# Talking-heads attention and a two-layer feed-forward: VectorE's order in an attention step, block timing, and where 48 weight pieces are decoded

## The chip, the cores and the metric

The kernel runs on one core of one Trainium2 chip, in one launch. The metric is the device time of that launch in microseconds; the lower the better. Each run also leaves a profile of one execution, taken on the same core.

## What is computed

```python
# q, k, v: (4, 12, 448, 64); w_pre, w_post: (12, 12)
scores = np.matmul(q, k.transpose(0, 1, 3, 2)) / np.sqrt(64)
scores = np.einsum('bhij,hg->bgij', scores, w_pre)
scores = scores - np.max(scores, axis=-1, keepdims=True)
attn = np.exp(scores)
attn = attn / (np.sum(attn, axis=-1, keepdims=True) + 1e-09)
attn = np.einsum('bhij,hg->bgij', attn, w_post)
out = np.matmul(attn, v)
x = out.transpose(0, 2, 1, 3).reshape(1792, 768)
h = x @ w_in                                   # w_in: (768, 2048)
g = np.where(h > 0, h, np.exp(np.minimum(h, 0)) - 1)
y = g @ w_out                                  # w_out: (2048, 768)
```

The two feed-forward weights arrive as 64-bit floats, the rest as 32-bit floats.

## The kernel before

**Attention.** The 448 query rows of a batch are cut into four blocks of 9, 12, 12 and 12 groups of 10 rows. With 12 heads, one group fills 120 partitions, so that the mixing over heads (w_pre, w_post) is a 120 x 120 product. Steps `j` take two groups each: a block is 5 or 6 steps, and 92 steps make the four batches. In one pass of the loop over `j` these things are issued, in the order in which they stand in the code, and each engine works through its own share in that order (the attention is under `manual_schedule`):

- `norm` for the step that was scored one pass earlier: the reciprocal of the sums on VectorE (L210, L211, tile `rz`) and two scalings of w_post on GpSimd (L215, tile `wz`).
- `scores` for step `j + 2`: two products `s` (L198) from the block's `raw` tile, VectorE's maxima `nm` (L200), ScalarE's exponentials `p` with their sums (L202).
- on some passes a *unit*: the q x k products of two head pairs for a coming block (L179), copied by ScalarE and VectorE into `st` (L187) and sent by a DMA into that block's `raw` tile, which changes the layout (L189). A block needs three units. `AHEAD` says how many steps ahead of the block's first scores its last unit stands.
- on some passes `av`: the products with v of a block that is already normalised (L249), and VectorE's copy `x` of the result (L261); the third one's DMA writes the block to DRAM (`xd`, L265).
- `post` for step `j`: two products with `wz` (L224, tile `t`), copied by ScalarE into `at` (L235).
- `dec.step()`: one of four VectorE operations of the weight decoder (below).
- work that is planned for this pass: loads of q, k and v, and their split into a high and a low part (L148, L149, L160, L161).

**Decoder.** Class `Weights` turns a 64-bit float into a 32-bit one by integer operations, in pieces of 128 x 512 numbers; 24 pieces make w_in (`s1`) and 24 make w_out (`s2`). A piece takes a load (`w`, L54), four VectorE operations in four calls of `step` (L68, L71, L77, L80), one ScalarE square (L75), and a store into DRAM (L84). The first `EARLY` pieces are decoded in the attention, where GpSimd issues the DMAs, the others in the feed-forward, where SyncE does.

**Feed-forward.** Two halves of 896 tokens. In each half the first products run over 16 slices `f` of the 2048 hidden columns and two groups of 448 tokens `u`, which gives 32 *units* of 18 products of 128 x 128 by 448 (L397). VectorE, ScalarE and VectorE again make the activation (L401, L403, L404, L405, L406), and ScalarE and GpSimd split it into `gh` and `gl` (L407, L408). The second products `y` follow (L445): 12 groups of 48. For every `f` and every group the weights are loaded from DRAM (L382), split by ScalarE into `hi` (L384) and by GpSimd into `lo` (L385). Before the first unit the tokens are loaded (`xl`, L367) and split into `xh` and `xl` (L369, L370). The decoder's calls stand in the first half only. The feed-forward is not under `manual_schedule`: the compiler's scheduler orders its instructions on each engine, and the order in the code is only its input.

Of the kernel before, what the change touches and what calls it, by code (L numbers as in the profile page):

```python
# [27 lines left out]
NC = DM // 128  # L28
PW = 512
EPS = 1e-9  # L30
EARLY = 22
LATE = 2


def f32(ap):
# [58 lines left out]
def body(ctx, tc, qd, kd, vd, wpre, wpost, w1d, w2d, outT):  # L94
# [5 lines left out]
    with tc.manual_schedule():  # L100
        attention(tc, qd, kd, vd, wpre, wpost, xd, todo[:EARLY])
    moe(tc, xd, s1, s2, todo[EARLY:], outT)


@with_exitstack
def attention(ctx, tc, qd, kd, vd, wpre, wpost, xd, todo):
    nc = tc.nc
# [18 lines left out]
    dec = Weights(ctx, tc, todo, nc.gpsimd)  # L126

    blocks = [(b, i) for b in range(B) for i in range(NB)]
    NBL = len(blocks)
# [4 lines left out]
    first = [steps.index((n, [0, 1])) for n in range(NBL)]  # L134
    length = [(c + 1) // 2 for c in count]
# [16 lines left out]
    def load_q(n, eng):  # L152
        q2[n] = ld.tile([128, NP, 120], F32, tag="q2", name="q2")
        eng.dma_start(out=q2[n], in_=qd[blocks[n]])

    def split_q(n, high, low):
        src = q2.pop(n)
        qh = qp.tile([128, NP, 120], F32R, tag="qh", name="qh")
        ql = qp.tile([128, NP, 120], F32R, tag="ql", name="ql")
        high(qh, src)  # L160
        low.tensor_sub(ql, src, f32(qh))  # L161
        qs[n] = qh, ql

    def load_v(b, hp):
        vs[b, hp] = vp.tile([128, NJ, 128], F32, tag="v", name="v")[:CJ]
        nc.gpsimd.dma_start(out=vs[b, hp], in_=vd[b, hp])
# [16 lines left out]
    def keep_qk(n, hp, got):  # L183
        m = count[n] * R
        for hh, copy in enumerate((nc.scalar.copy, nc.vector.tensor_copy)):
            st = stp.tile([120, S], F32, tag="st", name="st")
            copy(st[:m], got[hh][:m, :S])  # L187
            eng = nc.gpsimd if n == 0 and hh else nc.sync
            eng.dma_start(out=raws[n][2 * hp + hh:RH:H, :count[n], :], in_=st[:m])  # L189
# [17 lines left out]
    def norm(got, z):  # L207
        k = len(got)
        rz = small.tile([RH, 2], F32, tag="rz", name="rz")
        nc.vector.tensor_scalar_add(rz[:, :k], z[:, :k], EPS)  # L210
        nc.vector.reciprocal(rz[:, :k], rz[:, :k])  # L211
        out = []
        for i, p in enumerate(got):
            wz = small.tile([RH, RH], F32, tag="wz", name="wz", bufs=5)
            nc.gpsimd.tensor_scalar_mul(wz, wb, rz[:, i:i + 1])  # L215
            out.append((p, wz))
        return out
# [59 lines left out]
    wb = cst.tile([RH, RH], F32, name="wb")  # L277
    nc.sync.dma_start(out=wa, in_=wpre)
    nc.sync.dma_start(out=wb, in_=wpost)
    load_q(1, nc.sync)  # L280
    split_q(0, nc.scalar.copy, nc.vector)
    for hp in range(NP + 1):
        if hp < NP:
            split_k(0, hp, nc.scalar.copy, nc.vector)
        if hp:
            keep_qk(0, hp - 1, qk(0, hp - 1))
    nc.vector.tensor_scalar_mul(wa, wa, 1.0 / float(np.sqrt(D)))
    split_q(1, nc.vector.tensor_copy, nc.gpsimd)

    LOOK = 2
    AHEAD = 2
    work, units, avs = {}, {}, {}

    def plan(j, f):
        work.setdefault(max(j, -LOOK), []).append(f)

    for n in range(1, NBL):
        b, i = blocks[n]  # L300
        at = [max(first[n] - LOOK - AHEAD - (2 - u) * length[n - 1] // 3, -LOOK) for u in range(3)]
        for u in range(3):
            units.setdefault(at[u], []).append((n, u))
        if n > 1:
            plan(at[0] - 6, lambda n=n: load_q(n, nc.gpsimd))
            plan(at[0] - 2, lambda n=n: split_q(n, nc.vector.tensor_copy, nc.gpsimd))
        if i == NB - 1 and b + 1 < B:
            for hp in range(NP):
                plan(at[hp // 2] - 3 + hp % 2, lambda b=b + 1, hp=hp: load_k(b, hp, nc.gpsimd))
                plan(at[hp // 2] + hp % 2, lambda b=b + 1, hp=hp: split_k(  # L310
                    b, hp, nc.vector.tensor_copy, nc.gpsimd))
    for n in range(NBL):
        b, i = blocks[n]
        for u in range(3):
            j = first[n] + length[n] + (u * length[n + 1] // 3 if n + 1 < NBL else u)
            avs.setdefault(j, []).append((n, u))
            if i == NB - 1 and b + 1 < B:
                for hp in (2 * u, 2 * u + 1):
                    plan(j + 1, lambda b=b + 1, hp=hp: load_v(b, hp))
    for hp in range(NP):  # L320
        plan(hp - 1, lambda hp=hp: load_v(0, hp))

    sc, nz = {}, {}
    for j in range(-LOOK, N + 3):
        if j + LOOK - 1 in sc:
            nz[j + LOOK - 1] = norm(*sc.pop(j + LOOK - 1))
        if 0 <= j + LOOK < N:
            sc[j + LOOK] = scores(*steps[j + LOOK])
        for n, u in units.get(j, ()):
            got = [qk(n, hp) for hp in (2 * u, 2 * u + 1)]  # L330
            for w in range(2):
                keep_qk(n, 2 * u + w, got[w])
        for n, u in avs.get(j, ()):
            for w in range(2):
                av(n, 2 * u + w)
            keep_av(n, u)
        if j in nz:
            keep_post(*steps[j], post(nz.pop(j)))
        if j >= LATE:
            dec.step()  # L340
        for f in work.get(j, ()):
            f()
    while dec.step():
# [4 lines left out]
def moe(ctx, tc, xd, s1, s2, todo, outT):  # L348
    nc = tc.nc
# [10 lines left out]
    dec = Weights(ctx, tc, todo, nc.sync)  # L360
# [59 lines left out]
    for half in range(2):  # L420
        if half == 0:
            ahead(0)
        xs = [load_x(2 * half + u) for u in range(2)]
        for f in range(NF):
            ahead(i + 1)
            wh, wl = ready.pop(i)
            i += 1
            for u in range(2):
                up(f, u, wh, wl, *xs[u])
            if half == 0:  # L430
                dec.step(5)
        for m in range(NC):
            y = [ps.tile([128, 512], F32, tag="ps", name="y")[:, :S] for u in range(2)]
            for e in range(2):
                if half == 0:
                    dec.step(5 if m < NC - 2 else 64)
                ahead(i + 1)
                wh, wl = ready.pop(i)
                i += 1
                for u in range(2):  # L440
                    for k in range(8):
                        f = e * 8 + k
                        ks = slice(k * 128, (k + 1) * 128)
                        for n, (w, g) in enumerate(((wh, gh), (wl, gh), (wh, gl))):
                            nc.tensor.matmul(  # L445
                                y[u], w[:, ks], g[f][:, u, :],
                                start=f == 0 and n == 0, stop=f == NF - 1 and n == 2)
            for u in range(2):
                o = op.tile([128, S], F32, tag="o", name="o")
                nc.scalar.copy(o, y[u])  # L450
                nc.sync.dma_start(
                    out=outT[m * 128:(m + 1) * 128, (2 * half + u) * S:(2 * half + u + 1) * S],
                    in_=o)
# [46 lines left out]
```

## Time and profile before

| | |
|---|---|
| device time, median of 3 runs | 1026.11 us (1019.07 to 1030.36) |
| profiled execution, its own time | 1019.95 us, span 1018.2 us |
| mean granted TensorE clock | 0.976 of full speed |
| busy: TensorE, VectorE, ScalarE, GpSimd | 940.9, 523.9, 475.5, 416.5 us |
| attention | about 0 to 505 us |
| first half: first products, second products | about 506 to 661, 661 to 781 us |
| second half: first products, second products | about 781 to 898, 898 to 1014 us |

A line of a group names the source line, engine and operation, then what is written from what is read with the shape, how often it stands there, the busy time, the mean of one, and the idle time of that engine just before it with what ended most of it. The products are pipelined and their ends are modelled, so a single product's duration is longer than its share of a train; the share is read from the length of the train.

### The profile page before, as it was taken

What the parts mean: (1) busy time and instruction counts of PE and PEld (TensorE: products, weight loads), DVE (VectorE), ACT (ScalarE), POOL (GpSimd) and SP (SyncE); (2) the same over time, 40 slices, a digit from 0 to 9 for tenths busy, and PEclk for the clock granted to TensorE, in tenths of its full rate; (3) what the DMA queues carried; (4) which work ended last, traced back from release to release, by engine and by line L of the source; (5) the groups of instructions that cost most, each with busy time, mean ns of one, the idle gap of its engine ahead of it and who ended that gap; (6) DMA issues with size and microseconds to landing.
All of it is one profiled execution on the core that took longest, in us unless ns stands there. A gap on an engine that the chain in (4) does not pass through costs nothing.

```text
span 1018.2 us, 17108 instructions
## 1 busy us (share of the span) xinstructions
PE 940.9 (92%) x6216; PEld 775.3 (76%) x6216; DVE 523.9 (51%) x957; ACT 475.5 (47%) x988; POOL 416.5 (41%) x443
## 2 busy tenths in 40 slices
PE   4899999999999998999889888899999999999998
PEld 1576776677766666667778777789999999999997
DVE  3465665665556665555489999981001555530000
ACT  3465565565656565565545444552111555531110
POOL 2445434463445533333225444453222565641220
PEclk8899999999999999999989889999999999999999
DMA  5655436653565434642555455572221212122120
GB/s 178 193 170 163 140 127 191 188 181 119 174 215 173 145 126 159 201 140 83 151 191 182 156 171 170 178 210 94 80 81 62 62 47 63 52 71 89 62 87 28
DMA packets 78361, 136.30 MB, mean 134 GB/s; under 512 B 22894, under 2 KB 51890, under 8 KB 78278
## 3 DMA queue, kind: packets, MB, share of 16 engines
q1 hardware_dynamic: 68230, 101.23, 31.4%
q0 software_dynamic: 9504, 33.07, 10.6%
q8 instruction: 50, 0.82, 0.3%
q10 hardware_dynamic: 544, 0.92, 0.2%
q14 instruction: 33, 0.27, 0.1%
HBM read 72.86 MB, written 23.62 MB: 95 GB/s over the span
## 4 chain that ended last, share of the span: by engine, by line
PE 73%; DVE 14%; DMA 5%; issue 4%; ACT 3%; POOL 1%; SPq 0%; DVEq 0%; ACTq 0%; POOLq 0%
PE y L445 22%; PE s L198 13%; PE t L224 12%; PE h L397 12%; PE t L249 7%; PE qk L179 7%; DMA raw<-st 4%; DVE c L71 2%; DVE g L405 2%; DVE c L68 2%; DVE c L77 2%; DVE g L406 1%; DVE c L80 1%; DVE g L401 1%; ACT at L235 1%
## 5 line engine op out<-in xcount | busy, mean ns | idle before, releaser
L385 POOL TENSOR_TENSOR lo<-lo,hi 128x768 fp32r<-128x768 f32 (+1 forms) x56 | 119.4, 2134 | 205.3 <-ACT hi L384 205.1
L224 PEld LDWEIGHTS t<-wz,p 120*112 120x112 f32 x1440 | 158.4, 177 | 39.7 <-issue 35.0
L215 POOL TENSOR_SCALAR wz<-wb,rz 120x120 f32<-120x120 f32 x180 | 108.1, 609 | 182.7 <-DVE rz L211 174.9
L224 PE MATMUL t<-wz,p 120*112 120x120 f32 x1440 | 170.8, 270 | 12.6 <-ACT at L235 12.6
L198 PE MATMUL s<-raw,wa 120*120 120x448 f32 x360 | 156.1, 556 | 25.8 <-DMA raw<-st 11.2
L200 DVE TENSOR_REDUCE nm<-s 120x1 f32<-120x448 f32 x180 | 112.0, 624 | 127.7 <-PE s L198 117.4
L397 PE MATMUL h<-xh,hi 128*128 128x448 f32 x384 | 145.0, 378 | 17.3 <-ACT hi L384 11.0
L202 ACT ACTIVATE p<-s,nm 120x448 f32<-120x448 f32 x180 | 114.1, 634 | 100.2 <-DVE nm L200 97.1
L397 PE MATMUL h<-xh,lo 128*128 128x448 f32 x384 | 145.2, 378 | 7.1 <-POOL lo L385 7.0
L235 ACT COPY at<-t 112x480 f32<-112x480 f32 x180 | 96.2, 559 | 110.3 <-PE t L224 110.3
L397 PE MATMUL h<-xl,hi 128*128 128x448 f32 x384 | 144.1, 375 | 0.5 <-DMA lo<-s 0.5
L445 PE MATMUL y<-gh,lo 128*128 128x448 f32 x384 | 140.4, 366 | 2.1 <-POOL lo L385 2.1
L445 PE MATMUL y<-gh,hi 128*128 128x448 f32 x384 | 140.4, 366 | 0.4 <-ACT hi L384 0.4
L445 PE MATMUL y<-gl,hi 128*128 128x448 f32 x384 | 140.4, 366 | 0.2 <-POOL gl L408 0.2
L408 POOL TENSOR_TENSOR gl<-g,gh 128x448 fp32r<-128x448 f32 x64 | 86.0, 1344 | 85.5 <-ACT gh L407 82.1
L384 ACT CAST hi<-lo 128x768 fp32r<-128x768 f32 (+1 forms) x56 | 51.8, 925 | 129.3 <-DMA lo<-s 127.9
L198 PEld LDWEIGHTS s<-raw,wa 120*120 120x120 f32 x360 | 59.3, 186 | 65.3 <-issue 44.6
L397 PEld LDWEIGHTS h<-xh,hi 128*128 128x128 f32 x384 | 74.9, 195 | 25.7 <-ACT hi L384 12.9
L401 DVE TENSOR_SCALAR g<-h 128x448 f32<-128x448 f32 x64 | 39.6, 620 | 103.0 <-PE h L397 97.5
L397 PEld LDWEIGHTS h<-xh,lo 128*128 128x128 f32 x384 | 74.8, 195 | 16.9 <-POOL lo L385 10.7
L249 PEld LDWEIGHTS t<-at,v 112*64 112x64 f32 x1536 | 74.2, 136 | 16.4 <-issue 13.1
L249 PE MATMUL t<-at,v 112*64 112x120 f32 (+1 forms) x1536 | 84.1, 262 | 1.0 <-ACT at L235 1.0
(49 smaller groups left out, 1221.8 us busy)
## 6 DMA issues: line engine op xcount, KB each, us to landing
raw<-st SPq DMA_DIRECT2D x144, 210.0 KB
lo<-s SPq DMA_DIRECT2D x80, 256.0 KB
w<-in SPq DMA_DIRECT2D x26, 512.0 KB
w<-in POOLq DMA_DIRECT2D x22, 512.0 KB, 5.3
s<-c SPq DMA_DIRECT2D x26, 256.0 KB
raw<-st SPq DMA_DIRECT2D x42, 157.5 KB
s<-c POOLq DMA_DIRECT2D x22, 256.0 KB, 3.2
v<-in POOLq DMA_DIRECT2D x24, 224.0 KB, 4.5
```

The lines of the kernel that those rows point to most:

```text
L179: nc.tensor.matmul(got[hh][:m, :S], q[part, hp, :m], k[part], start=i == 0, stop=i == 2)
L198: nc.tensor.matmul(ps[:RH, :S], wa, raws[n][:RH, t, :], start=True, stop=True)
L200: nc.vector.tensor_reduce(nm, ps[:RH, :S], op=ALU.max, axis=AX.X, negate=True)
L202: nc.scalar.activation(p, ps[:RH, :S], AF.Exp, bias=nm, scale=1.0, accum_out=z[:, i:i + 1])
L215: nc.gpsimd.tensor_scalar_mul(wz, wb, rz[:, i:i + 1])
L224: nc.tensor.matmul(ps[:CJ, c * RH:(c + 1) * RH], p[:, c * CJ:(c + 1) * CJ], wz, start=True, stop=True,)
L235: nc.scalar.copy(ats[n][:, :, t, :], ps[:CJ, :NJ * RH].rearrange("p (c n) -> p c n", c=NJ))
L249: nc.tensor.matmul(ps[hh * 64:(hh + 1) * 64, w * m:(w + 1) * m].rearrange("p (t r) -> p t r", r=R), vs[blocks[n][0], hp][:, c, hh * 64:(hh ...
L385: nc.gpsimd.tensor_sub(lo_[:, :done], f32(lo_[:, :done]), f32(hi_[:, :done]))
L397: nc.tensor.matmul(h, w[:, ks], x[:, k, :], start=n == 0, stop=n == 3 * NC - 1)
L408: nc.gpsimd.tensor_sub(gl[f][:, u, :], g, f32(gh[f][:, u, :]))
L445: nc.tensor.matmul(y[u], w[:, ks], g[f][:, u, :], start=f == 0 and n == 0, stop=f == NF - 1 and n == 2)
```

## The change

- In a pass of the attention `norm` stands behind `scores` and the unit, so VectorE does maxima, copies, reciprocals.
- A block's units stand one step earlier (`AHEAD` 3 for 2), its `av` one step later; q is loaded 4 steps ahead of the first unit and not 6; the first v loads stand one step later; the load of the second block's q moves from SyncE's queue to GpSimd's, behind the first block's `raw` DMAs.
- `EARLY` is 30 for 22. The decoder starts at step 3 and makes two operations in every third step.
- In the feed-forward's code one decoder operation stands behind each slice `f`, and seven stand ahead of each group of second products.

```diff
-EARLY = 22
-LATE = 2
+EARLY = 30
+LATE = 3
...
-    load_q(1, nc.sync)
     split_q(0, nc.scalar.copy, nc.vector)
...
+    load_q(1, nc.gpsimd)
     split_q(1, nc.vector.tensor_copy, nc.gpsimd)
...
-    AHEAD = 2
+    AHEAD = 3
...
-            plan(at[0] - 6, lambda n=n: load_q(n, nc.gpsimd))
+            plan(at[0] - 4, lambda n=n: load_q(n, nc.gpsimd))
...
-            j = first[n] + length[n] + (u * length[n + 1] // 3 if n + 1 < NBL else u)
+            j = first[n] + length[n] + (1 + u * length[n + 1] // 3 if n + 1 < NBL else u)
...
-        plan(hp - 1, lambda hp=hp: load_v(0, hp))
+        plan(hp, lambda hp=hp: load_v(0, hp))
...
-        if j + LOOK - 1 in sc:
-            nz[j + LOOK - 1] = norm(*sc.pop(j + LOOK - 1))
         if 0 <= j + LOOK < N:
             sc[j + LOOK] = scores(*steps[j + LOOK])
         for n, u in units.get(j, ()):
             got = [qk(n, hp) for hp in (2 * u, 2 * u + 1)]
             for w in range(2):
                 keep_qk(n, 2 * u + w, got[w])
+        if j + LOOK - 1 in sc:
+            nz[j + LOOK - 1] = norm(*sc.pop(j + LOOK - 1))
...
         if j >= LATE:
-            dec.step()
+            dec.step(1 + (j % 3 == 0))
...
             if half == 0:
-                dec.step(5)
+                dec.step()
...
                 if half == 0:
-                    dec.step(5 if m < NC - 2 else 64)
+                    dec.step(7)
```

**The start of the attention, on VectorE.** From the first maxima (L200) on the rows of before are these; every L187 row is a unit of the second block:

```order
L200 TENSOR_REDUCE nm<-s 120x1 x2
L187 COPY st<-qk 120x448 x2
L210 TENSOR_SCALAR rz<-z 120x2
L211 RECIPROCAL rz<-rz 120x2
L200 TENSOR_REDUCE nm<-s 120x1 x2
L210 TENSOR_SCALAR rz<-z 120x2
L211 RECIPROCAL rz<-rz 120x2
L200 TENSOR_REDUCE nm<-s 120x1 x2
L187 COPY st<-qk 120x448 x2
```

The same place of the change:

```order
L200 TENSOR_REDUCE nm<-s 120x1 x2
L187 COPY st<-qk 120x448 x2
L200 TENSOR_REDUCE nm<-s 120x1 x2
L187 COPY st<-qk 120x448 x2
L210 TENSOR_SCALAR rz<-z 120x2
L211 RECIPROCAL rz<-rz 120x2
L200 TENSOR_REDUCE nm<-s 120x1 x2
L187 COPY st<-qk 120x448 x2
```

The reciprocals stand behind maxima and copies, and the second block's units stand in the first three passes. Before they stood in the first, third and fourth, of which the last lies behind these rows.

**The start of the feed-forward, on ScalarE.** Here `xh` is made for the two groups of tokens, and `gh` for the first unit. Before:

```order
L369 CAST xh<-xl 128x448 x6
L403 ACTIVATE e<-g 128x448
L404 ACTIVATE g<-g 128x448
L407 CAST gh_5870<-g 128x448
L369 CAST xh<-xl 128x448 x6
```

Of the change:

```order
L369 CAST xh<-xl 128x448 x6
L403 ACTIVATE e<-g 128x448
L404 ACTIVATE g<-g 128x448
L369 CAST xh<-xl 128x448 x6
L384 CAST hi<-lo 128x768
L407 CAST gh_5950<-g 128x448
```

The second group's split no longer stands behind `gh`. On SyncE the loads of `xl` moved too: before, the last two of each group stood behind a store of the attention's result (`xd`, L265); of the change only the very last one does.

**VectorE around the 22nd to 24th of the 32 units of the first half's first products.** Before (L401 opens a unit, L405 and L406 close it, L68 to L80 are the decoder; the 22nd unit's L401 is the first row):

```order
L401 TENSOR_SCALAR g<-h 128x448
L68 TENSOR_SCALAR c<-w 128x512
L71 SCALAR_TENSOR_TENSOR c<-w,c 128x512
L77 SCALAR_TENSOR_TENSOR c<-w,c 128x512
L405 SCALAR_TENSOR_TENSOR g<-e,g 128x448
L401 TENSOR_SCALAR g<-h 128x448
L406 TENSOR_TENSOR g<-g,h 128x448
L80 SCALAR_TENSOR_TENSOR c<-sq,c 128x512
L68 TENSOR_SCALAR c<-w 128x512
L71 SCALAR_TENSOR_TENSOR c<-w,c 128x512
```

Of the change, from the 22nd unit's L401 too:

```order
L401 TENSOR_SCALAR g<-h 128x448
L406 TENSOR_TENSOR g<-g,h 128x448
L77 SCALAR_TENSOR_TENSOR c<-w,c 128x512
L405 SCALAR_TENSOR_TENSOR g<-e,g 128x448
L80 SCALAR_TENSOR_TENSOR c<-sq,c 128x512
L406 TENSOR_TENSOR g<-g,h 128x448
L401 TENSOR_SCALAR g<-h 128x448
L405 SCALAR_TENSOR_TENSOR g<-e,g 128x448
L406 TENSOR_TENSOR g<-g,h 128x448
L401 TENSOR_SCALAR g<-h 128x448
```

The L80 in the rows of the change is that of its 48th and last piece; behind it the list holds units alone. At the first of these rows 18 pieces are finished in this stage before, and eight are to come, up to the 32nd unit. Of the change 17 are finished there and two operations of the 18th. So the built program leaves no piece for the second products, before or of the change.

## Rows read from the trace of the kernel before

**Rows 1.** The page: the span, and the busy time of each engine with its share and its instructions.

```profile
span 1018.2 us, 17108 instructions
PE 940.9 (92%) x6216; PEld 775.3 (76%) x6216; DVE 523.9 (51%) x957; ACT 475.5 (47%) x988; POOL 416.5 (41%) x443
```

**Rows 2.** Busy time by stretch: the attention without its start, the first half's first products in two parts, its second products. Columns: the stretch and its length, busy time and instructions of each engine, granted TensorE clock, share and rate of the DMA engines.

```profile
50.00:498.00 448.00, 422.66 (x3669) 314.00 (x3669) 263.31 (x592) 259.26 (x620) 194.83 (x293) 0.99 0.50 157
...
515.00:628.00 113.00, 100.96 (x450) 88.84 (x450) 111.72 (x141) 55.61 (x98) 52.18 (x33) 0.92 0.51 163
628.00:661.00 33.00, 26.15 (x108) 22.29 (x108) 32.62 (x44) 16.11 (x28) 14.16 (x9) 0.90 0.55 179
...
661.00:781.00 120.00, 117.59 (x577) 108.26 (x578) 24.92 (x32) 32.54 (x52) 39.34 (x19) 1.00 0.36 109
```

**Rows 3.** The chain of work that ended last: the second half's first products, start, length and count.

```profile
781.05 116.73 PE h L397 x576
```

**Rows 4.** Waits from 50 to 498 us: who waited for whom, in total, how often, the longest.

```profile
PE t L224 <- ACT at L235: 12.6, 17, 0.7
...
PE s L198 <- DMA raw<-st: 6.8, 6, 1.9
...
PE s L198 <- issue: 2.6, 3, 1.8
...
PE s L198 <- ACT sq L75: 1.5, 1, 1.5
PE s L198 <- ACT at L235: 1.3, 2, 0.8
```

**Rows 5.** TensorE in order of time, at the first scores of the second and the third block: start, length, what, and in brackets the idle time before it with what ended it.

```profile
46.84 3.34 PE L198 MATMUL s<-raw,wa 120*120 120x448 f32 x4 [4.35 <-DMA raw<-st]
...
77.96 2.48 PE L198 MATMUL s<-raw,wa 120*120 120x448 f32 x4 [1.91 <-DMA raw<-st]
```

**Rows 6.** The chain of waits, a light step (scores and post alone) and the products of a heavy one (a unit, an av and a post as well): start, length, what, count.

```profile
127.21 1.50 PE s L198 x4
128.71 1.64 PE t L224 x16
...
131.86 1.38 PE qk L179 x12
133.24 1.79 PE t L249 x32
135.03 1.82 PE t L224 x16
```

**Rows 7.** VectorE's decoder operations in the attention, 50 to 498 us, by line: count, busy time, mean ns of one, idle time before them.

```profile
L80 DVE SCALAR_TENSOR_TENSOR c<-sq,c 128x512 f32<-128x512 f32 x22 | 15.6, 711 | 0.0
L77 DVE SCALAR_TENSOR_TENSOR c<-w,c 128x512 int32<-128x512 int32 x22 | 15.5, 706 | 0.0
L71 DVE SCALAR_TENSOR_TENSOR c<-w,c 128x512 int32<-128x512 int32 x22 | 15.2, 690 | 0.0
...
L68 DVE TENSOR_SCALAR c<-w 128x512 int32<-128x512 int32 x22 | 9.6, 436 | 0.0
```

**Rows 8.** VectorE's work in the first half's first products, 515 to 690 us, by line, in the same columns.

```profile
L71 DVE SCALAR_TENSOR_TENSOR c<-w,c 128x512 int32<-128x512 int32 x26 | 32.0, 1229 | 0.6
L80 DVE SCALAR_TENSOR_TENSOR c<-sq,c 128x512 f32<-128x512 f32 x26 | 26.6, 1024 | 0.3
L77 DVE SCALAR_TENSOR_TENSOR c<-w,c 128x512 int32<-128x512 int32 x26 | 26.5, 1021 | 0.6
L405 DVE SCALAR_TENSOR_TENSOR g<-e,g 128x448 f32<-128x448 f32 x31 | 22.9, 740 | 1.4 <-ACT g L404 1.3
L68 DVE TENSOR_SCALAR c<-w 128x512 int32<-128x512 int32 x26 | 22.4, 862 | 0.3 <-DMA s<-c 0.3
L401 DVE TENSOR_SCALAR g<-h 128x448 f32<-128x448 f32 x31 | 19.1, 615 | 0.0
L406 DVE TENSOR_TENSOR g<-g,h 128x448 f32<-128x448 f32 x31 | 18.9, 611 | 0.1
```

**Rows 9.** The feed-forward's first two units in order of time: SyncE's issue of the second group's last two loads, ScalarE's split of that group, TensorE's first product with it.

```profile
506.75 1.26 SPq L367 DMA_DIRECT2D xl<-xd  x2
...
514.11 2.89 ACT L369 CAST xh<-xl 128x448 fp32r<-128x448 f32 x6
...
514.72 0.74 PE L397 MATMUL h<-xh,hi 128*128 128x448 f32 x1 [4.35 <-ACT xh L369]
```

**Rows 10.** TensorE and ScalarE in order of time, late in the first half's first products and at the first of its second products: where TensorE found a weight slice not yet split.

```profile
629.53 0.83 ACT L384 CAST hi<-lo 128x768 fp32r<-128x768 f32 x1 [1.64 <-DMA lo<-s]
...
630.42 0.47 PE L397 MATMUL h<-xh,hi 128*128 128x448 f32 x1 [3.05 <-ACT hi L384]
632.37 0.74 PE L397 MATMUL h<-xh,lo 128*128 128x448 f32 x1 [1.27 <-POOL lo L385]
...
663.71 0.47 PE L445 MATMUL y<-gh,lo 128*128 128x448 f32 x1 [2.14 <-POOL lo L385]
```

**Rows 11.** One heavy attention step, VectorE and GpSimd: GpSimd's two scalings of w_post, VectorE's two maxima, its two copies.

```profile
150.57 1.14 POOL L215 TENSOR_SCALAR wz<-wb,rz 120x120 f32<-120x120 f32 x2 [2.81 <-DVE rz L211]
...
150.86 1.38 DVE L200 TENSOR_REDUCE nm<-s 120x1 f32<-120x448 f32 x2 [0.48 <-PE s L198]
...
152.44 1.23 DVE L187 COPY st<-qk 120x448 f32<-120x448 f32 x2 [0.21 <-PE qk L179]
```

## The prediction

> **What bounds the kernel now.** I read the page first. TensorE is busy 940.9 of 1018.2 us and VectorE 523.9 [rows 1]. Such shares are averages over stages with different limits, so next come the stretches [rows 2]. The second half's first products show a stage that TensorE alone limits: 576 products in 116.73 us [rows 3], so 0.2027 us for a product in a full train and 3.65 us for a unit of 18. The same work in the first half has other limits. From 515 to 661 us VectorE is busy 144.34 of 146 us (the two rows added), while TensorE issues 558 products, which at 0.2027 us would take 113.1 us. So 32.9 us are lost there, and VectorE sets the pace: 26 decoder pieces stand between the 32 units. One piece costs 1.229 + 1.024 + 1.021 + 0.862 = 4.14 us of VectorE, one unit 0.740 + 0.615 + 0.611 = 1.97 us [rows 8]. TensorE feels it through ScalarE's and GpSimd's splits of the next weights, which stand behind that work in their queues: it waits 3.05 us for `hi` and 1.27 us for `lo` [rows 10].
>
> In the attention TensorE is close to full: busy 422.66 of 448 us, with VectorE at 263.31 [rows 2]. Its 25.3 us of idle time have three sources [rows 4]: 12.6 us for a `t` buffer that ScalarE has not emptied, 6.8 + 2.6 us at the first scores of a block (the 2.6 us, listed as issue, stand at the same place, ahead of `s`), and 1.5 + 1.3 us where maxima or exponentials are late. Ahead of that stretch the second block's first scores wait 4.35 us for their `raw` DMA, and then run for 3.34 us, where four such products take 1.50 us at full speed [rows 5, 6], as at the lower of the clock's two levels (1.2 for 2.4 GHz).
>
> **The change part by part.** The sum is made against the profiled execution, 1019.95 us.
>
> *Units one step earlier.* At the attention's start the second block's last unit moves ahead by one pass, so its DMAs leave at least a light step earlier: 1.50 + 1.64 = 3.14 us [rows 6], and the pass before it now carries the next block's unit, 1.38 us more. That is 4.5 us against a wait of 4.35 us [rows 5]. The slow clock behind it costs up to 3.34 - 1.50 = 1.84 us. Bounds: 0 (the DMA engines set the landing) to 6.2. I take 5. At the later blocks the slack grows by a heavy step, 1.38 + 1.79 + 1.82 + 1.50 = 6.5 us [rows 6], and the longest wait is 1.9 us [rows 4], so all 9.4 us should go. Bounds: 0 to 10.4, with 2.48 - 1.50 us of slow clock at the third block [rows 5]. I take 9.
>
> *VectorE's order.* Maxima no longer stand behind reciprocals that wait for an exponential or for GpSimd. This can win the 1.5 + 1.3 us [rows 4]. It puts `rz`, and so `wz`, later by the maxima and copies, 1.38 + 1.23 = 2.6 us [rows 11]; GpSimd's 1.14 us follow. `wz` is wanted by the next pass, a light step of 3.14 us or a heavy one of 6.5 us later, and behind the next scores (1.50 us). A pass with copies is heavy, so the later `rz` still leads by more than 2 us. I take a gain of 1; bounds: a gain of 2.8, a loss as in the rivals.
>
> *Eight more pieces in the attention.* A piece there costs 0.711 + 0.706 + 0.690 + 0.436 = 2.54 us of VectorE [rows 7], 20.3 us in all. The cover is VectorE's idle time of 448 - 263.31 = 184.7 us [rows 2]. GpSimd issues sixteen more DMAs beside 194.83 us of work in 448. What leaks out are places where double operations and the casts of a new batch meet: I take a cost of 2; bounds 0 to 20.3, if the cover were gone. The `t` wait stays: in the built order it stands at 18 places, before at 17, so 12.6/17 = 0.7 us more.
>
> The rows on the decoder deserve a second look. L71 takes 690 ns in the attention and 1229 ns in the first products [rows 7, 8], on the same operands; GpSimd's large subtractions run beside the second. The Trainium skill, SBUF — State Buffer, section SBUF: two separate sides, says that VectorE and GpSimd share a port pair as an exclusive lock held for a whole instruction, and that a VectorE operation with two SBUF inputs needs it against a GpSimd operation that reads SBUF. By that rule the moved decoding could in turn hold up GpSimd's scalings; the two prices of L71 agree with it, and no row shows TensorE waiting for a scaling so held. At the dearer price of [rows 8] the eight pieces would be 8 x 4.14 = 33.1 us of VectorE, still under the cover, so the sum stays.
>
> *Start of the feed-forward.* TensorE waits 4.35 us for the second group's `xh`, whose split began at 514.11, behind the first unit's `gh` and behind loads issued at 506.75 [rows 9]. In the new order it stands ahead of `gh`, and only the last load waits for the attention's last store. I take 2.5; bounds 0 to 4.35.
>
> *First products.* The words of the change place most remaining pieces in the second products. The built order does not: all 18 stand between the first and the 22nd unit, as dense as before. So up to there VectorE keeps its pace, and is ahead by two operations of a piece, 1.024 + 1.021 = 2.0 us [rows 8]. Behind it the list holds units alone, at 1.97 us of VectorE against 3.65 us of TensorE, and TensorE takes over. At 628 us it has 108 products, six units, to go, which took 33 us [rows 2] and need 6 x 3.65 = 21.9. With about 2 us left for the refill (the waits of [rows 10] are 4.3 us): 33 - 21.9 - 2 + 2.0 = 11. Bounds: 5 (the tail halves its loss only) to 32.9 (the whole loss).
>
> *Second products, first half.* TensorE idles 120 - 117.59 = 2.4 us there [rows 2], 2.14 us of it at a `lo` that stood behind the decoding [rows 10]. I take 2; bounds 0 to 2.4.
>
> Sum: -5 - 9 - 1 + 2 + 0.7 - 2.5 - 11 - 2 = -28, so 992 us for an execution like the profiled one. That execution lies 6.2 us below the median of 1026.11. I add half of that: 995.
>
> **The rivals.**
>
> *Only the feed-forward gains.* If the `raw` waits follow the DMA engines (share 0.50 in the attention) and the added pieces' 6 MB (8 x 768 KB by the tiles' sizes) delay them as much as the earlier issue helps, the attention's -12 falls away: 995 + 12 = 1007. A second way to about the same end is a scaling held by a decoder operation: 24 more two-input operations of about 0.70 us [rows 7] give back 17 us, 1012, if each falls on TensorE's path. That is what the Trainium skill's rule on the shared port, named above, would do at its worst. For the first way: eight pieces add loads. Against: waits of at most 1.9 us meet 6.5 us of slack, and `wz` has about 2 us.
>
> *The first products come loose earlier.* The stage's loss of 32.9 us feeds on itself, since each wait is followed by a low clock (0.92 and 0.90 granted). If the missing piece and the earlier start break that, another 10 to 20 us go: 975 to 985. Against: the density of decoding up to unit 22 is unchanged.
>
> *Slower: `wz` becomes the wait.* With the reciprocals behind copies, GpSimd gets `rz` late, and every post waits. The slack is about 2 us; past it each 0.1 us costs 92 x 0.1 = 9 us. At a shortfall of 0.35 us a step the 28 us are gone, beyond that the kernel is slower; at 0.5 us it takes 995 + 46 = 1041. For it: 2.6 us of shift. Against: GpSimd is busy under half the time, and heavy steps last 6.5 us.
>
> *VectorE late in the double steps.* Every third step carries two decoder operations, up to 1.4 us. If 31 such steps each delay the next maxima by about 0.9 us, the gain is 28 too small: about 1020.
>
> **How the numbers follow.** Forecast, 985 to 1004 on the median's scale: 0.55. Feed-forward alone, 1004 to 1014: 0.17. Looser first products, 970 to 985: 0.14. VectorE late, 1014 to 1036: 0.09. Slower by `wz`: 0.05. A measurement of this kernel can tell about 1% from no change, 10.3 us, so faster ends at 1015.8. Faster: 0.55 + 0.17 + 0.14 = 0.86; same 0.09; slower 0.05. The range that leaves out 0.2 is 978 to 1014: it drops the slow cases (0.14) and the far end of the loose one.
>
> **What would show it.** Right: no idle time before `s` with a DMA as its end in the attention; the attention over about 15 us earlier; the first half's first products still at the old pace until about their 22nd unit, with VectorE at 99%, and then trains without waits; no decoding after that. Wrong: TensorE waiting for `wz`; `s` waiting for exponentials more often; the first products' last six units still taking 33 us; or decoding inside the second products, which would mean that the built order was read wrongly.

## The result, and the profile after

The changed kernel takes 993.31 us (median of 4 runs, 992.01 to 995.60) beside 1028.23 us for the kernel before on the same chip (4 runs, 1019.07 to 1033.62). The ratio is 0.967, with a 95% interval of 0.960 to 0.975. The forecast was 995, its range 978 to 1014. The profiled execution took 992.42 us, its span is 990.6 us against 1018.2 [rows 1]. Runs over 1.5% above the fastest of their kernel (one each in experiments 1 and 11) count in the medians below, but not in the ratios.

The page's first rows: TensorE's busy share rises because the span shrinks, and GpSimd's work grows. PE is TensorE, PEld its loading of weights, DVE is VectorE, ACT ScalarE, POOL GpSimd, and SPq SyncE's queue.

```profile
span 990.6 us, 17065 instructions
PE 932.3 (94%) x6216; PEld 773.0 (78%) x6216; DVE 517.3 (52%) x957; ACT 475.6 (48%) x988; POOL 444.0 (45%) x460
```

The stages, read off the two traces (us; the start of the first feed-forward product, of the first second product, of the second half):

| | first product | first `y` | second half | span |
|---|---|---|---|---|
| before | 506.45 | 661.10 | 780.89 | 1018.2 |
| after | 489.27 | 636.55 | 753.28 | 990.6 |
| stage shorter by | 17.2 | 7.4 | 3.1 | (sum 27.6) |

The forecast had 12.3 for the attention (its terms -5, -9, -1, +2, +0.7), 13.5 for the first products and their start (-2.5, -11), and 2 for the second products. The sum, 28, is right; two of its parts are not.

The waits of the attention, 40 to 480 us (who for whom, total, how often, longest). The waits of `s` for a raw DMA [rows 4, 5] are gone, the wait for a `t` buffer stays, and the wait of 4.1 us is new:

```profile
PE t L224 <- ACT at L235: 11.8, 16, 0.7
PE s L198 <- ACT p L202: 4.1, 1, 4.1
PE t L224 <- POOL wz L215: 1.5, 2, 0.7
```

The two waits under `wz` last 0.74 us each, like every wait for `t`, and stand where experiment 4 has two of its 18 waits for `t` (68.84 and 148.88 us there, 74.75 and 154.77 here). So they are most likely waits for `t` too.

In order of time, on GpSimd, VectorE and TensorE, the new wait:

```profile
45.33 1.16 POOL L54 DMA_DIRECT2D w<-in  x2
...
51.59 0.43 DVE L68 TENSOR_SCALAR c<-w 128x512 int32<-128x512 int32 x1 [6.99 <-DMA w<-in]
51.93 1.15 DVE L200 TENSOR_REDUCE nm<-s 120x1 f32<-120x448 f32 x2
...
53.36 3.00 PE L198 MATMUL s<-raw,wa 120*120 120x448 f32 x4 [4.13 <-ACT p L202]
```

The change starts the decoder at step 3, which is also a step with two operations: the load of the first piece and the operation that reads it stand in one step. VectorE waits 6.99 us with the next maxima queued behind it, and the products that follow run 3.00 us in place of 1.50 [rows 6].

The feed-forward's start (TensorE): the wait of 4.35 us for `xh` [rows 9] is 2.39 us.

```profile
495.65 0.47 PE L397 MATMUL h<-xh,hi 128*128 128x448 f32 x1 [2.39 <-ACT xh L369]
497.05 0.47 PE L397 MATMUL h<-xl,hi 128*128 128x448 f32 x1 [0.93 <-DVE xl L370]
...
602.87 0.47 PE L397 MATMUL h<-xh,hi 128*128 128x448 f32 x1 [3.55 <-ACT hi L384]
605.62 0.74 PE L397 MATMUL h<-xh,lo 128*128 128x448 f32 x1 [1.98 <-POOL lo L385]
```

Then the chain of work that ended last shows one train to the end of the stage, and the second products without a wait:

```profile
605.62 31.09 PE h L397 x142
636.71 116.73 PE y L445 x576
```

And in the stretches (length, busy time of PE, PEld, DVE, ACT, POOL, granted clock, DMA share and rate) VectorE is the pace only up to that train:

```profile
495.00:605.00 110.00, 93.65 (x416) 82.75 (x416) 108.62 (x135) 54.78 (x96) 50.51 (x32) 0.91 0.50 162
605.00:637.00 32.00, 31.38 (x145) 28.93 (x146) 21.48 (x30) 17.33 (x29) 17.89 (x13) 0.92 0.34 107
```

### The profile page after: what moved, and what is told of

Read it like the earlier page. It is cut to its first block, busy times and chain, and to the rows that moved or that the text cites. A ratio compares the mean times of both kernels' runs of the same rounds, so it can differ in the third digit from the quotient of the medians.

```text
span 990.6 us, 17065 instructions
## 1 busy us (share of the span) xinstructions
PE 932.3 (94%) x6216; PEld 773.0 (78%) x6216; DVE 517.3 (52%) x957; ACT 475.6 (48%) x988; POOL 444.0 (45%) x460
## 3 DMA queue, kind: packets, MB, share of 16 engines
q1 hardware_dynamic: 65782, 94.56, 30.7%
q0 software_dynamic: 11376, 39.73, 13.3%
## 4 chain that ended last, share of the span: by engine, by line
PE 85%; DVE 6%; issue 3%; DMA 2%; ACT 2%; POOL 1%; SPq 0%; DVEq 0%; POOLq 0%; ACTq 0%
PE y L445 24%; PE h L397 18%; PE t L224 16%; PE s L198 14%; PE t L249 8%; PE qk L179 6%; DVE c L71 1%; DVE g L405 1%; DMA raw<-st 1%; ACT at L235 1%; DVE c L77 1%; DVE g L406 1%; DVE g L401 1%; DMA w<-in 1%; DVE c L68 1%
## 5 line engine op out<-in xcount | busy, mean ns | idle before, releaser
L215 POOL TENSOR_SCALAR wz<-wb,rz 120x120 f32<-120x120 f32 x180 | 128.0, 718 | 189.9 <-DVE rz L211 173.2
L224 PE MATMUL t<-wz,p 120*112 120x120 f32 x1440 | 171.8, 270 | 13.3 <-ACT at L235 11.8
L198 PE MATMUL s<-raw,wa 120*120 120x448 f32 x360 | 153.8, 550 | 12.1 <-DMA raw<-st 7.9
L200 DVE TENSOR_REDUCE nm<-s 120x1 f32<-120x448 f32 x180 | 111.8, 624 | 101.9 <-PE s L198 91.7
L408 POOL TENSOR_TENSOR gl<-g,gh 128x448 fp32r<-128x448 f32 x64 | 82.9, 1295 | 72.2 <-ACT gh L407 72.2
L401 DVE TENSOR_SCALAR g<-h 128x448 f32<-128x448 f32 x64 | 39.6, 618 | 106.6 <-PE h L397 101.4
```

The source lines that it names most:

```text
L198: nc.tensor.matmul(ps[:RH, :S], wa, raws[n][:RH, t, :], start=True, stop=True)
L200: nc.vector.tensor_reduce(nm, ps[:RH, :S], op=ALU.max, axis=AX.X, negate=True)
L224: nc.tensor.matmul(ps[:CJ, c * RH:(c + 1) * RH], p[:, c * CJ:(c + 1) * CJ], wz, start=True, stop=True,)
L408: nc.gpsimd.tensor_sub(gl[f][:, u, :], g, f32(gh[f][:, u, :]))
```

## The experiments

Twelve kernels ran. Ratios are to the kernel before on the same chip; first product means the start of the feed-forward's first product in the profiled execution (506.45 before, 489.27 after). Runs of one kernel differ by 2 to 17 us, so a few us are read from the traces, not from medians.

**1. VectorE's order undone in the changed kernel.**

```diff
+        if j + LOOK - 1 in sc:
+            nz[j + LOOK - 1] = norm(*sc.pop(j + LOOK - 1))
         if 0 <= j + LOOK < N:
             sc[j + LOOK] = scores(*steps[j + LOOK])
...
-        if j + LOOK - 1 in sc:
-            nz[j + LOOK - 1] = norm(*sc.pop(j + LOOK - 1))
```

> The changed kernel with norm put back ahead of scores, so VectorE again does reciprocals, maxima, copies; everything else as changed. Theory (the forecast): the order of VectorE carries at most about 1 to 3 us of the 35, so 993 to 997 us, and the first feed-forward product starts 0 to 3 us later than at 489.27. Rival A (the order carries the attention's gain): 1003 us or more, with exponentials or maxima late on TensorE again. The built order of the feed-forward is the same as in the changed kernel, so a difference can only come from the attention.

997.82 us, ratio 0.973 (0.967 to 0.979); first product at 497.88. The intervals overlap with that of the changed kernel. Of the 8.6 us at the first product 2.05 lie ahead of the first scores. A raw wait of 2.3 us and exponentials late by 5.8 us in four places (for 4.1 in one) are back. That execution took 1001.08 us; two of the other three took 994.07 and 994.56, as long as the changed kernel. So with units that stand early no run settles what the order is worth, and it does not carry the attention's gain.

**2. AHEAD undone in the changed kernel.**

```diff
-    AHEAD = 3
+    AHEAD = 2
```

> The changed kernel with AHEAD 2 for 3: each block's units stand one step later, as before; the later av, the loads and the rest as changed. Theory: the early units took 14 us of the attention (waits of s for raw DMAs and the slow clock behind them), so 1005 to 1010 us, and s waits for raw again for 8 to 14 us in total. Rival A (VectorE's order made the gain): about 993. Rival B (the later av or the loads made it): about 993 too, with no wait for raw.

1047.52 us, ratio 1.022 (1.017 to 1.027), slower than the kernel before; first product at 539.04. Neither theory nor rivals had this: AHEAD is worth 54 us in the changed kernel and not 14, so something else in the change costs dearly when the units stand late. TensorE's waits from 26 to 539 us begin:

```profile
PE s L198 <- DMA raw<-st: 11.6, 4, 3.8
PE s L198 <- issue: 8.9, 5, 3.5
```

The clock granted in the same stretch is 0.96, for 0.99 in the kernel before from 26 to 506 us.

**3. The decoder's move undone.** 22 pieces, one operation a step, the feed-forward's calls as before.

```diff
-EARLY = 30
-LATE = 3
+EARLY = 22
+LATE = 2
...
-            dec.step(1 + (j % 3 == 0))
+            dec.step()
...
-                dec.step()
+                dec.step(5)
...
-                    dec.step(7)
+                    dec.step(5 if m < NC - 2 else 64)
```

> The changed kernel with the decoder as before: 22 pieces in the attention, one operation a step from step 2, 26 pieces in the feed-forward with its calls as before; VectorE's order and the block timing as changed. Theory: the first half's first products and its second products lose the 7 + 3 us that they gained, and the attention loses the new 4.1 us wait for the first decoder load and its slow clock: 996 to 1000 us; first product to first y about 154 us, attention 4 to 6 us shorter. Rival C (the decoder move made most of the gain, in the attention too): 1010 us or more.

1001.31 us, ratio 0.978 (0.972 to 0.983). First product at 487.74, 1.5 us earlier; first products 149.35 us, second products 121.84. So the move costs the attention 1.5 and gives 2.1 + 5.1 us in the feed-forward. That is 7.2 us there for the expected 10, with the shares of the two stages the other way round, and 1.5 in the attention for the expected 4 to 6. The profiled execution, 998.05 us, lies in the expected range, the median 1.3 us above it.

**4. The first decoder operation two steps behind its load.**

```diff
-        if j >= LATE:
-            dec.step(1 + (j % 3 == 0))
+        if j >= LATE and j != 4:
+            dec.step(1 + (j % 3 == 0 and j > 3))
```

> The changed kernel with the first decoder load at step 3 as changed, but its first operation at step 5 and not in the same step, so that VectorE does not wait for that load with the next maxima behind it. Theory: the 7.0 us wait of VectorE ahead of its first decoder operation and the 4.1 us wait of TensorE for exponentials behind it go, with the 1.5 us of slow clock after them: 987 to 990 us. Rival (TensorE then waits for the second block's raw DMAs at the same place): 991 to 994 us, with s waiting for a DMA at about 49 us.

994.14 us (988.61 to 998.34), ratio 0.969 (0.963 to 0.976): no difference that can be measured. In the trace the wait is gone, and so is the slow train behind it; no raw wait took its place, so the rival fell too. The first product comes at 487.36, 1.9 us earlier, where the wait and the slow train are 5.6; waits of 1.56 and 2.58 us stand later on (the second is 1.93 in the changed kernel). What the profiled execution lost elsewhere is told in the last section.

**5 and 6. AHEAD 2, and one more part undone.** First the av's place, then the decoder as in experiment 3.

```diff
-    AHEAD = 3
+    AHEAD = 2
...
-            j = first[n] + length[n] + (1 + u * length[n + 1] // 3 if n + 1 < NBL else u)
+            j = first[n] + length[n] + (u * length[n + 1] // 3 if n + 1 < NBL else u)
```

> The changed kernel with AHEAD 2 and with each block's av in the steps of before, so that a unit and an av share a step again (with AHEAD 2 alone they stand in alternate steps). It tells why AHEAD 2 alone cost 54 us and not 14. Theory M (unit and av must share a step, the alternation of light and heavy steps hides the DMA): 1003 to 1012 us, no wait for raw over 2 us. Theory D (the eight added pieces' DMAs make the raw transfers land later, whatever step the av stands in): 1030 us or more, with waits of s for raw of 2 to 4 us at several blocks and a granted clock of 0.90 to 0.97 behind them.

> The changed kernel with AHEAD 2 and with the decoder as before (22 pieces in the attention, one operation a step, 26 in the feed-forward), the av one step later as changed. Theory D (the added pieces' DMAs): waits for raw shrink to 2 us or less, no slow clock, 1010 to 1018 us. Theory M (unit and av in alternate steps): the waits and the slow clock stay, 1045 us or more, as with AHEAD 2 alone plus the 8 us that the decoder as before costs.

1036.81 (ratio 1.013, 1.006 to 1.019) and 1036.93 us (1.013, 1.008 to 1.017); first product at 535.27 and 526.32. Each undoing gives 11 us back, and neither removes the waits of 2 to 5 us at a block's first scores. The first time speaks against M and lies where D would have it; the second, with no added piece, lies above D's bounds and below M's. So neither theory, as stated, holds for both, and the waits do not need the added pieces.

**7 and 8. More pieces in the attention.**

```diff
-EARLY = 30
+EARLY = 38
...
-        if j >= LATE:
-            dec.step(1 + (j % 3 == 0))
+        if j >= LATE and j != 4:
+            dec.step(1 if j == LATE else 1 + (j % 4 != 0))
```

With 48 pieces the last line ends in `2 + (j % 6 == 0)`.

> The changed kernel with 38 pieces decoded in the attention for 30 (two operations in three steps of four, the first decoder operation two steps after its load); ten pieces are left for the first products, where the built order has them up to the 13th unit for the 22nd. The first products still lose 30 us against 116.7. Theory E (the loss lasts as long as decoding stands between the units): it falls in proportion, 30 x 9/22 = 12 us less there, and the attention gives back 1 to 4: 982 to 988 us. Rival W (VectorE's work alone sets it, 8 x 4.1 us): the first products fall to about 118 us, 965 us. Rival D (the attention pays: raw waits and slow clock come back with the added DMAs): 1000 us or more.

> The changed kernel with all 48 pieces decoded in the attention (two operations in every step, three in every sixth), none in the feed-forward. Theory E: the first products fall from 147 to 118 to 122 us (-26 to -29); VectorE in the attention takes 18 x 2.5 = 46 us more under about 150 us of idle time, which costs 3 to 10 us: 968 to 980 us. Rival D (the DMAs of 18 more pieces delay the raw transfers): s waits for raw at most blocks with slow clock behind, attention 30 us or more longer, 1000 us or more. Rival V (VectorE late with maxima in every step, 92 x 0.3 us): about 995 us.

With 38 pieces 971.75 us (971.10 to 972.87), ratio 0.948 (0.944 to 0.951): faster than both kernels. First product at 481.16, first products 127.5 us, 20 less than after, between E and W. The attention paid nothing: it is 8.1 us shorter than in the changed kernel (this kernel has the edit of experiment 4 too). Its stretch (columns as above) shows TensorE full with the DMA engines at 0.64, and the chain one train of 250 products ahead of the second products:

```profile
50.00:480.00 430.00, 415.10 (x3715) 311.10 (x3713) 302.29 (x654) 267.02 (x630) 235.93 (x327) 1.00 0.64 197
```

```profile
556.91 51.93 PE h L397 x250
608.84 119.04 PE y L445 x576
```

With 48 pieces 988.31 us, ratio 0.966 (0.960 to 0.972). The first products fall to 122.4 us, about as expected, but the attention takes 30 us more than with 38. There is no raw wait (D fell); TensorE waits for VectorE's copies and, behind late maxima, for exponentials, from 26 to 511 us:

```profile
PE t L224 <- DVE x L261: 7.2, 5, 2.7
PE s L198 <- ACT p L202: 6.5, 6, 1.8
PE t L249 <- DVE x L261: 5.2, 1, 5.2
```

These waits are 18.9 us. V named the engine, but VectorE isn't late because it has too much to do: from 50 to 480 us it is busy 307.6 of 430 us, with 38 pieces 302.3. It stands still for DMAs, from 26 to 511 us:

```profile
DVE x L261 <- DMA xd<-x: 26.9, 7, 7.7
...
DVE c L68 <- DMA w<-in: 19.8, 8, 5.4
```

There is one `x` buffer, so a block's first copy waits until the store of the block before has landed (14.5 us in all with 38 pieces, 3.7 at most). Behind the three longest of these waits, 7.7, 5.9 and 6.0 us, TensorE waits 0.5 to 2.7 us for `x` and 1.6 to 1.8 us for exponentials. Its 5.2 us stand behind the 5.4 us for the last piece's load. No run here gives VectorE a second `x` buffer or issues the loads earlier, so how much of the 30 us that would give back is open.

**9. AHEAD 2, and the loads as before.** To experiment 2 this is added:

```diff
+    load_q(1, nc.sync)
...
-    load_q(1, nc.gpsimd)
...
-            plan(at[0] - 4, lambda n=n: load_q(n, nc.gpsimd))
+            plan(at[0] - 6, lambda n=n: load_q(n, nc.gpsimd))
...
-        plan(hp, lambda hp=hp: load_v(0, hp))
+        plan(hp - 1, lambda hp=hp: load_v(0, hp))
```

> The changed kernel with AHEAD 2 and with the loads as before (q six steps ahead of its first unit, the second block's q on SyncE's queue, the first v loads one step earlier); the later av, VectorE's order and the decoder as changed. With AHEAD 2 alone the last raw DMA of a block landed up to 7.8 us behind its issue, where before it took 2.9 to 5.4 us. Theory L (the later q loads share the DMA engines with a block's last raw DMAs): the landings fall back to 5.5 us or less, waits for raw to 2 us or less, 1005 to 1020 us. Theory D' (it is the av's place or the added pieces, each of which alone made 11 us): landings of 6 to 8 us stay, 1035 us or more.

1041.75 us, ratio 1.019 (1.010 to 1.027); first product at 534.91. A raw DMA's landing is not in the trace; where scores wait for it, it is read here from their start, and counted from the end of the last raw DMA's issue. It took 6.5 to 8.0 us at five blocks. Theory L fell. What stood in all of 2, 5, 6 and 9 and not in the kernel before is VectorE's order.

**10. The kernel before with AHEAD 3 alone.** The edit of experiment 2 the other way round, in the kernel before.

> The kernel before with AHEAD 3 for 2 and nothing else. The forecast's own term for it: the raw waits of 4.35 + 9.4 us go, -14, so 1010 to 1014 us, with no wait for raw after the first block's. Theory 2 (a longer lead of about 10 us saves also the waits and low clocks that vary from execution to execution; unit and av now fall into alternate steps, which costs nothing): -15 to -22, 1004 to 1011 us. Rival (unit and av must share a step): 1020 us or more.

1005.00 us, ratio 0.983 (0.976 to 0.990), that is 10 to 24 us gained. The medians differ by 15.4. In the profiled pair the first product comes 20.9 us earlier, at 485.53; the profiled execution, 999.22 us, is the shortest of the four. TensorE's waits for raw and the clock in the attention:

```profile
PE t L224 <- ACT at L235: 9.6, 13, 0.7
...
PE s L198 <- DMA raw<-st: 0.5, 1, 0.5
```

```profile
50.00:480.00 430.00, 419.22 (x3664) 306.37 (x3662) 254.44 (x586) 265.07 (x615) 190.74 (x294) 1.00 0.52 165
```

From 25 us on the kernel before waits 11.2 + 2.6 us at a block's first scores, and the 1.5 + 1.3 us under "ACT sq" and "ACT at" [rows 4] go with the same edit: 16.6 less the 0.5 left, and 3.0 us of waits for `t`. Theory 2 holds; sharing a step is not needed.

**11. 44 pieces, two operations in every step and never three.** As experiment 7, with `EARLY = 44` and `2` for the last term.

> The changed kernel with 44 pieces decoded in the attention, exactly two operations in every step from step 5, four pieces left for the first products (built order: up to their 5th unit). With 48 pieces the attention took 510.9 us to the first product for 481.2 with 38, and every sixth step held three operations. Theory V3 (the steps with three operations make VectorE late): attention 481 to 490 us, first products 121 to 124 us, 965 to 973 us in all. Rival V2 (two operations in every step are too many already, with x copies and maxima late): attention 500 us or more, 980 us or more.

973.21 us (967.85 to 985.08), ratio 0.951 (0.944 to 0.958). First product at 490.17, first products 122.05 us. Without the triple steps (and with four pieces fewer) the attention is 20.7 us shorter than with 48; it is still 9 longer than with 38, of which the first products give back 5.5. That is V3 at the upper edge of its bounds, but the triple steps and the four pieces are not told apart; 38 and 44 can't be told apart by their intervals.

**12. The kernel before with VectorE's new order alone.** The edit of experiment 1 the other way round.

> The kernel before with norm behind scores and the unit, and nothing else: VectorE does maxima, copies, reciprocals, with AHEAD 2. The forecast's own term: -1 (bounds -2.8 and 0), 1017 to 1021 us beside a kernel before of 1020. Theory O (with AHEAD 2, where the kernel changed but for AHEAD took 1047 us and undoing the av, the loads or the decoder left 1037 to 1042: later reciprocals make GpSimd's scalings late, and the decoder's DMAs that stand behind them in GpSimd's queue then leave together with a block's last raw DMAs, which land 5 to 8 us behind their issue for 3 to 5): 1030 to 1042 us, first feed-forward product at 520 us or later. Rival (the order is harmless, the slower kernels come from two or more of the other parts together): 1010 to 1024 us.

1038.77 us, ratio 1.013 (1.008 to 1.019): slower, and theory O holds. First product at 527.72, 21.3 us later, in the longest of its four runs; the medians differ by 16. One block shows how. In the kernel before, around the last unit of the fifth block (GpSimd's queue, SyncE's raw DMAs of that unit, the scores):

```profile
130.86 1.14 POOL L215 TENSOR_SCALAR wz<-wb,rz 120x120 f32<-120x120 f32 x2 [3.78 <-DVE rz L211]
131.95 0.58 POOL L84 DMA_DIRECT2D s<-c  x1
132.53 0.55 POOL L54 DMA_DIRECT2D w<-in  x1
...
133.78 3.31 SPq L189 DMA_DIRECT2D raw<-st  x4
...
140.15 1.36 PE L198 MATMUL s<-raw,wa 120*120 120x448 f32 x3 [0.15 <-issue]
```

With the order alone:

```profile
137.62 1.14 POOL L215 TENSOR_SCALAR wz<-wb,rz 120x120 f32<-120x120 f32 x2 [3.15 <-DVE rz L211]
138.70 0.58 POOL L84 DMA_DIRECT2D s<-c  x1
139.29 0.55 POOL L54 DMA_DIRECT2D w<-in  x1
...
137.00 3.31 SPq L189 DMA_DIRECT2D raw<-st  x4
...
146.77 2.79 PE L198 MATMUL s<-raw,wa 120*120 120x448 f32 x4 [3.54 <-DMA raw<-st]
```

The store and the load of a piece (768 KB) stand behind `wz` in GpSimd's queue, and `wz` waits for the reciprocals, which now stand behind the copies. Before they left 1.8 and 1.2 us ahead of the unit's first raw DMA; now they leave among its four, and the last of these lands 6.5 us behind the end of its issue, instead of 3.1 at most. It is so at each of the four blocks where the piece's DMAs leave less than 2 us ahead of the last raw DMA's end of issue (first scores wait 4.1, 3.5, 5.0 and 4.0 us, before 1.9, 0.2, 0.6 and 1.5); at the other blocks behind the first two the waits are 0.0 to 2.3 us. Experiments 2, 5, 6 and 9 show the same: in each there are four blocks where the piece's DMAs leave 1.7 to 3.5 us behind the unit's first raw DMA, and at all 16 the first scores wait 2.0 to 5.0 us. Some waits of up to 3.7 us at other blocks behind the first two of those kernels have another origin, which was not looked for. Each long wait is followed by products at the lower clock: four `s` in 2.79 us, a granted clock of 0.91 from 140 to 160 us. The Trainium skill, DMA: Bandwidth & Descriptors, section Issuing engines are not separate DMA queues, says that transfers started by different engines run on the same 16 DMA engines and interleave; the 6.5 us for 3.1 agree with it. So theory D had the right transfers and the wrong reason: this kernel has no piece more than before, and what differs is when their DMAs leave. That the DMAs cause the late landings is read from these blocks; no run moves them alone.

## Why the prediction was right, point by point

The sum came out as near as it did partly by luck: the attention gave about 5 us more than its terms, the feed-forward about 5 less.

**Units one step earlier, 5 + 9 of 28.** Right mechanism, shown by experiment 10. The size is open: the medians give 15.4 us (10 to 24), the profiled pair 20.9. The forecast left out waits that stood under other names at the same first scores (2.8 us), which it gave to the order, and 3.0 us of `t` waits that went too. After the change the last raw DMA of most blocks is issued some 10 us ahead of the scores, before 3 to 5. The changed kernel's attention gains 17.2 us. Experiment 3 puts the eight pieces at 1.5, experiment 4 the early decoder operation at 1.9; but with 38 pieces the attention is shorter than in any other run, so such small differences between single executions settle little.

**VectorE's order, 1.** The step that failed. The forecast followed the later `rz` to `wz` and to TensorE's next post, found 2 us of slack, and stopped. That part held: under `wz` stand only the two waits of 0.74 us that are most likely waits for `t`. But behind `wz` in GpSimd's queue stand DMAs, and it did not ask what they meet. With AHEAD 2 the order alone is a loss of 16 us (experiment 12); with AHEAD 3 its undoing costs 4.5 by the medians, which is inside the spread of the runs (experiment 1). The forecast's number came out near because the change brings AHEAD 3 too. So the terms don't add up: 1005 with AHEAD alone, 1039 with the order alone, and the changed kernel has both.

**The rival on scalings held by decoder operations.** The page shows a mean `wz` of 718 ns for 609 before. The Trainium skill, SBUF — State Buffer, section SBUF: two separate sides, says that VectorE and GpSimd hold their shared port pair as an exclusive lock for a whole instruction; the longer scalings agree with it, the more so since experiment 1, with as many decoder operations but the old order, has 609 ns from 50 to 480 us. But experiment 12, with the decoder of before and the new order, has 684 there, so it is the order that makes them longer, and not the added pieces that the rival blamed. It cost TensorE nothing that a row shows.

**Eight more pieces, +2; the `t` wait, +0.7; start of the feed-forward, -2.5.** The pieces: 1.5 (experiment 3), with the new wait in it. The `t` waits: 16 and most likely the two under `wz`, 13.3 us for 12.6, as forecast. The start: about 2 (4.35 to 2.39 us at `xh`). The pieces kept their price of [rows 7], L71 with 676 ns for 690. "VectorE late in the double steps" fell at this density. With 48 pieces VectorE is late, but behind DMAs (experiment 8).

**First products, -11.** Over-sized; the stage, its start included, gives 7.4 for 13.5. The built order was read rightly: all 18 pieces stand in the stage, at the old pace, and a free train follows. VectorE's rows from 489 to 637 us are near the prices of [rows 8], 4.25 us a piece for 4.14:

```profile
L80 DVE SCALAR_TENSOR_TENSOR c<-sq,c 128x512 f32<-128x512 f32 x18 | 22.4, 1243 | 0.1
L71 DVE SCALAR_TENSOR_TENSOR c<-w,c 128x512 int32<-128x512 int32 x18 | 21.8, 1209 | 0.3
L77 DVE SCALAR_TENSOR_TENSOR c<-w,c 128x512 int32<-128x512 int32 x18 | 18.9, 1049 | 0.3
...
L68 DVE TENSOR_SCALAR c<-w 128x512 int32<-128x512 int32 x18 | 13.4, 746 | 0.0
```

The last 108 products take 21.9 us for 30.7 before, 8.8 less where the forecast's step had 9.1. What failed is the assumption that TensorE enters the tail ahead by 2.0 + 2.5 us. It enters it 1.4 us later than before (product 469 starts 125.4 us behind the first, before 124.0), though product 397 still starts 3.6 us earlier than before (101.7 for 105.3): in between lie the 3.55 + 1.98 us for the 13th slice's `hi` and `lo`, shown above, where the forecast left about 2 for the refill. Experiment 3 tells the pieces apart from the rest: they give 2.1 us in the first products and 5.1 in the second, 7.2 for the forecast's 11 + 2; the other 3.2 us of the feed-forward's gain came without them.

**Second products, -2.** 3.1 measured; the stage runs without a wait.

## What to carry to other kernels

When an operation is put later on an engine, follow everything that its queue issues behind it, DMAs too, and ask which transfers these will now meet. The same reordering lost 16 us where the transfer that it met had 3 to 5 us of lead, and lost nothing that the runs show where it had some 10; give the critical transfer lead first. Work moved into a stage's idle engine is cheap up to a density that has to be found: 38 pieces cost the attention nothing, 48 cost it 30 us, and the limit need not be that engine's time: VectorE stood still for DMAs.

## What the hardware showed that was not expected

A train of 576 feed-forward products without a wait took 116.73 to 116.75 us in nine of the fourteen profiled executions and 119.04 to 119.05 in five (experiments 2, 4, 5, 7 and 9). The granted clock is 1.00 for both, as in this row of experiment 2 and the row of the changed kernel under it (columns as above):

```profile
806.00:924.00 118.00, 118.00 (x573) 107.18 (x572) 60.51 (x91) 64.26 (x109) 67.70 (x46) 1.00 0.19 58
```

```profile
754.00:870.00 116.00, 116.00 (x574) 107.53 (x573) 60.34 (x91) 63.83 (x109) 68.02 (x46) 1.00 0.20 59
```

That is 2.3 us in each of the three free stages, 6.9 us a kernel, and it hides the 1.9 us in the profiled execution of experiment 4. What sets the level was not tried. In the kernel before, waits of up to 1.8 us left the clock at full speed behind them (the 50 us slices from 100 to 500 us all at 1.00). Behind the wait of 1.91 us at 77.96 us four `s` took 2.48 us for 1.50 [rows 5, 6], and behind the waits of 3.5 to 5 us in experiment 12 they took 2.79 to 3.34.
